# The third slot's rows turned one product group earlier, in a fused attention and routed-expert kernel

## The chip, the cores and the metric

The kernel runs on one core of one Trainium2 chip. The metric is the device time of one execution in microseconds (us); less is better. The kernel before takes 415.35 us, the median of three runs (415.18 to 416.78).

## What is computed

Attention comes first: 4 batches, 8 heads, 768 positions of 64 elements, where a position sees the first 8 positions and the last 96, with a bias that falls with the distance. Its output, 3072 rows of 512, goes into a layer of 8 experts. Each row goes to the one expert with the largest logit:

```python
logits = x @ w_gate + modality_bias[modality_id]
e_idx = np.argmax(logits, axis=1)
...
for e in range(E):
    mask = e_idx == e
    h = np.maximum(x[mask] @ w1[e], 0.0)
    out[mask] = gate_w[mask, None] * (h @ w2[e])
```

w1 of an expert is 512 x 1024, w2 is 1024 x 512, all in float32.

## The kernel before

**Slots.** After attention the rows are worked on in eight slots, one after the other (`for u in range(nslot)`, line 1733). A slot is a set of rows that share an expert: `e0` and `e1` have 4 blocks of 128 rows, then come `p0` (4 blocks, the third slot, u = 2), `g0` (1), `p1` (4), `g1` (1), `p2` (4) and `u0` (2). Since float32 products are made of three products of rounded numbers, every operand is held as a high half and a low half (`xh`, `xl` for the rows, `ah`, `al` for w1, `bh`, `bl` for w2, `hh`, `hl` for the hidden layer).

**Groups.** A slot of four blocks has eight product groups, g = 0 to 7. In `l1` (line 799) a group makes 128 of the 1024 hidden columns for all 512 rows: 12 matmuls of 128x512 into one bank `ph` (lines 826 to 828), then ScalarE makes `hh` of it (line 829) and VectorE `hl` (line 830). In `l2` (line 841) the same hidden columns are multiplied by w2: 12 matmuls into four banks `po` (lines 854 to 856). The loop puts `l2` of a group behind `l1` of the next one, so TensorE does `l1(g)`, `l2(g-1)`, `l1(g+1)`, `l2(g)`, and so on. Banks for `ph` alternate between two (`p_x`, line 84).

**Rows for the next slot.** The rows come from HBM by indirect transfers that GpSimd issues (`gather_q`, line 700, issued at line 716): 128 rows x 128 columns each, four for a block, 16 for a slot. Two are issued at each `move()`. A block, once there, goes through two steps. `turn` (line 763) is one VectorE transpose of 32x32 squares, from `xg` to `xf`. `halves_of` (line 769) is one ScalarE rounding to `xh` (line 774) and one VectorE subtraction to `xl` (line 775). All four blocks of `xh` and `xl` must be there before the first group of the slot, because each of its matmuls takes all 512 rows.

**Order.** TensorE, ScalarE and VectorE run in the order in which the program is written (`manual_schedule`, lines 1429 and 1431). In a group the loop writes, among others: `l1` with its `hh` and `hl`; two splits of weights into halves (`run(2)`, lines 751 and 757); `l2` of the group before; and at its end `fill(u, g)` (line 1662), which turns and halves the next slot's blocks. So what `fill` writes in group g stands in ScalarE's and VectorE's queues ahead of `hh`, `hl` and the splits of group g + 1. The last group of a slot has two splits of w1 for the next slot's second half (`ahp010`, `ahp011` and their low halves here).

**The few rows.** During `e1` a small product for a handful of rows of another expert runs as well: `few_t` (VectorE transpose `xTf`), `few_l1` (`phf`, 32 short matmuls in group 6, followed by `hrf` on ScalarE), `few_ht` (`htf`, two transposes on TensorE in group 7, followed by `hTf`), and `few_l2` (`pof`, in group 1 of `p0`).

Of the kernel before, what the change touches and what calls it, by code (L numbers as in the profile page):

```python
# [38 lines left out]
NE, NPS, NUS, NGR = 2, 3, 1, 2  # L39
# [30 lines left out]
def moe_attention_kernel(  # L70
# [599 lines left out]
    def ld_x(s):  # L670
        n = P * s.nt
        so = nc.sync.value_load(s.o_src, min_val=0, max_val=E * NT)
        s.ui = idp.tile([P, 4, IDW], I32, tag="ui", name=f"ui{s.name}")
        ins = nc.sync.dma_start(s.ui[:, 0 : s.nt, :], ids[ds(so, n), :].rearrange("(p t) o -> p t o", t=s.nt))
        return ins

    def ld_q(s):
        n = P * s.nt
        so = nc.sync.value_load(s.o_src, min_val=0, max_val=E * NT)
        s.uq = idq.tile([P, 4, 4, IDW], I32, tag="uq", name=f"uq{s.name}")  # L680
        src = ids[ds(so, n), :].rearrange("(g i t) o -> i g (t o)", g=4, t=s.nt)
        for b in range(4):
            nc.sync.dma_start(
                s.uq[M * b : M * b + M].rearrange("p g t o -> p g (t o)")[:, :, 0 : s.nt * IDW], src
            )
# [77 lines left out]
    def turn(s, t):  # L763


        s.xf[t] = mp.tile([P, 4, 4, M], F32, tag="xf", name=f"xf{s.name}{t}", bufs=5)
        V.transpose(s.xf[t], s.xg[:, t, :].rearrange("p (g c j) -> p c g j", g=4, c=4))

    def halves_of(s, t):
        if t == 0:  # L770
            x_hl(s)
        xf = s.xf.pop(t).rearrange("p c g i -> p c (g i)")
        sl = slice(t * P, (t + 1) * P)
        nc.scalar.copy(s.xh[:, :, sl], xf)  # L774
        V.tensor_tensor(s.xl[:, :, sl], xf, s.xh[:, :, sl].bitcast(F32), ALU.subtract)
# [84 lines left out]
    def few_in(s):  # L860
        so = nc.sync.value_load(s.o_src, min_val=0, max_val=E * NT)
        s.ui = idp.tile([P, 2], I32, tag="uif", name="uif", bufs=1)
        for g in range(4):
            nc.sync.dma_start(s.ui[M * g : M * g + M, :], ids[ds(so, M), 0:2])
# [755 lines left out]
    def load_on():  # L1620
        nonlocal nload
        while nload - nfree < NRAW and nload < 8 * len(order):
            i = nload
            with tc.issue_after(v_last[0].ins):
                ld_w(order[i // 8], "ab"[i // 2 % 2], i // 4 % 2, i % 2)
            nload += 1
# [35 lines left out]
    def fill(u, g):  # L1662

        s = order[u]
        nx = order[u + 1] if u + 1 < len(order) else None
        if u or g:
            next(bg, None)
        if len(order) == NE and len(slist) == NPS + NUS + NGR and not writes:

            order.extend(slist[j] for j in ORDER)  # L1670
            nx = order[u + 1]
        while ahead[0] < min(len(order), u + 4):
            ld_x(order[ahead[0]])
            if ahead[0] == NE:
                few_in(fs[0])
                ld_q(order[NE])
            ahead[0] += 1
        load_on()
        if ahead[1] < min(ahead[0], u + (3 if u < NE else 4)):
            s2 = order[ahead[1]]  # L1680
            if s2.rows:
                gathers.extend((gather_x, s2, t) for t in range(s2.nt))
            else:
                if ahead[1] > NE:
                    ld_q(s2)
                gathers.extend((gather_q, s2, t, g) for t in range(2 * (ahead[1] < NE), s2.nt) for g in range(4))
            if ahead[1] == NE:
                gathers.insert(len(gathers) - 8, (few_x, fs[0]))
            ahead[1] += 1
        if nx is not None and s.nt == 4:  # L1690
            first = (0, 4)[u] if u < NE else 2
            if first < g <= first + nx.nt:
                next_rows(u, (g - first - 1,), halves_of)
            if first <= g < first + nx.nt:
                next_rows(u, (g - first,), turn)
            if g + 1 == s.groups < first + nx.nt + 1:
                next_rows(u, (nx.nt - 1,), halves_of)
            if nx.nt == 1 and g > 3:
                turn(order[u + 2], g - 4)
                if g == 7:  # L1700
                    order[u + 2].mx = mx[u % 2]
                    for t in range(4):
                        halves_of(order[u + 2], t)
# [14 lines left out]
    def next_rows(u, ts, *fs_):  # L1718

        nx = order[u + 1]  # L1720
        nx.mx = mx[(u + 1) % 2]
        for f in fs_:
            for t in ts:
                assert nx.got > t
                f(nx, t)
# [7 lines left out]
    for u in range(nslot):  # L1733
        s = order[u]
        per = s.groups // 2
        for g in range(s.groups):
# [6 lines left out]
            nx = order[u + 1] if u + 1 < len(order) else None  # L1743
# [25 lines left out]
            if not u or 0 < g < 7:  # L1769
                move()  # L1770
            fill(u, g)
            if s.nt == 1 and g:
                run(2)
# [116 lines left out]
```

## Time and profile before

| what | us |
|---|---|
| median of three runs | 415.35 |
| lowest and highest run | 415.18, 416.78 |
| the profiled execution, its own time | 414.16 |
| its span, from the first to the last instruction | 412.3 |
| TensorE busy in the span | 394.3 |
| VectorE, ScalarE, GpSimd busy | 267.2, 228.7, 190.0 |

The span is 1.86 us shorter than the time of its own execution. Busy times of different engines lie beside each other, so they don't add up. Start times below count from the beginning of the span. In names, `xhp` is the tile `xh` of a `p` slot, `phe` the bank `ph` of an `e` slot, and so on; L826 is line 826. "x<-y" is what is written and what is read.

### The profile page before, as it was taken

To read this page: it belongs to the slowest core of one execution; us is meant where nothing else is said; L and a number is where in the kernel's file an instruction comes from. 1 tells how busy PE (TensorE), PEld (TensorE's weight loads), DVE (VectorE), ACT (ScalarE), POOL (GpSimd) and SP (SyncE) were. 2 spreads that over 40 slices of the span, in tenths; PEclk is the share of its full clock that TensorE was granted. 3 is DMA by queue.
4 is the path that set the end of the run, shared out by engine and by line. 5 is a ranking of instruction groups with operands and counts; after the bars stand their busy time and mean duration, and the time that the engine had idled before them with its cause. 6 is when DMAs were issued, how large, how long until landed. Compare 5 with 4: busy or idle time off the path is not lost.

```text
span 412.3 us, 10964 instructions
## 1 busy us (share of the span) xinstructions
PE 394.3 (96%) x3900; PEld 328.6 (80%) x3900; DVE 267.2 (65%) x859; ACT 228.7 (55%) x609; POOL 190.0 (46%) x334
## 2 busy tenths in 40 slices
PE   8899999999989999999997999999999999999993
PEld 6688778787877788888875888888888888888992
DVE  7899889899897598897534324488444676443220
ACT  7998889898874443263422522297232685332511
POOL 7700042276876777067770657503777340000301
PEclk9999999999999999999996999999999999999997
DMA  8999999989668762325744373449844479220201
GB/s 245 336 347 301 343 308 323 283 284 343 229 174 281 279 208 88 105 83 169 244 142 128 114 251 134 149 153 305 300 165 140 137 241 328 94 84 2 101 4 57
DMA packets 47535, 82.49 MB, mean 200 GB/s; under 512 B 11295, under 2 KB 24479, under 8 KB 47472
## 3 DMA queue, kind: packets, MB, share of 16 engines
q1 hardware_dynamic: 41296, 68.68, 51.0%
q0 software_dynamic: 5632, 12.76, 9.3%
q8 instruction: 33, 0.54, 0.5%
q10 hardware_dynamic: 544, 0.26, 0.2%
q14 instruction: 30, 0.25, 0.2%
HBM read 68.19 MB, written 13.55 MB: 198 GB/s over the span
## 4 chain that ended last, share of the span: by engine, by line
PE 80%; ACT 7%; issue 5%; DVE 4%; DMA 1%; POOL 1%; SPq 0%; POOLq 0%; DVEq 0%
ACT pr L316 6%; PE php L826 6%; PE php L827 6%; PE s L285 6%; PE php L828 5%; PE pop L855 5%; PE pop L856 5%; PE pop L854 5%; PE pt L337 5%; PE x L376 4%; PE phe L826 3%; PE poe L854 3%; PE phe L827 3%; PE poe L855 3%; PE poe L856 3%
## 5 line engine op out<-in xcount | busy, mean ns | idle before, releaser
L316 ACT ACTIVATE pr<-sc,nmx 128x168 f32<-128x168 f32 (+1 forms) x192 | 79.7, 417 | 10.1 <-DVE nmx L305 9.9
L830 DVE SCALAR_TENSOR_TENSOR hlp<-php,hhp 128x512 fp32r<-128x512 f32 x24 | 16.6, 691 | 70.1 <-ACT hhp L829 70.1
L829 ACT ACTIVATE hhp<-php 128x512 fp32r<-128x512 f32 x24 | 14.3, 598 | 80.2 <-PE php L828 80.2
L716 POOL DMA_INDIRECT xgp<-x_rows,iqp x48 | 51.4, 1071 | 15.1 <-issue 11.8
L305 DVE CUSTOM_DVE_ANT_0 sc<-s,tbl 128x168 f32<-128x168 f32 (+1 forms) x192 | 49.9, 320 | 6.7 <-PE s L285 3.9
L285 PE MATMUL s<-kb,qt 64*64 64x168 f32 (+1 forms) x768 | 40.4, 312 | 3.9 <-ACT pT L345 2.9
L954 POOL DMA_INDIRECT out<-obp,oip x12 | 14.0, 1168 | 63.9 <-ACT obp L953 61.5
L826 PE MATMUL php<-xhp,ahp 128*128 128x512 f32 x96 | 38.8, 404 | 3.0 <-ACT xhp L774 3.0
L827 PE MATMUL php<-xlp,ahp 128*128 128x512 f32 x96 | 38.5, 401 | 0.0
L828 PE MATMUL php<-xhp,alp 128*128 128x512 f32 x96 | 38.4, 400 | 0.0
L285 PEld LDWEIGHTS s<-kb,qt 64*64 64x64 f32 x768 | 28.1, 135 | 12.3 <-ACT pT L345 6.1
L855 PE MATMUL pop<-blp,hhp 128*128 128x512 f32 x96 | 37.4, 390 | 0.0
L854 PE MATMUL pop<-bhp,hhp 128*128 128x512 f32 x96 | 37.4, 390 | 0.0
L856 PE MATMUL pop<-bhp,hlp 128*128 128x512 f32 x96 | 37.4, 389 | 0.0
L316 ACT ACTIVATION_READ_ACCUMULATOR pr<-sc,nmx 128x1 f32 x192 | 36.0, 188 | 0.0
L559 POOL DMA_INDIRECT ids_sorted<-tki,pi x24 | 25.4, 1058 | 22.4 <-PE x L376 8.9
L337 PE MATMUL pt<-ident,pr 128*128 128x128 f32 x272 | 35.2, 278 | 0.0
L337 PEld LDWEIGHTS pt<-ident,pr 128*128 128x128 f32 x272 | 29.4, 141 | 3.6 <-issue 1.9
L829 ACT ACTIVATE hhe<-phe 128x512 fp32r<-128x512 f32 x16 | 9.6, 597 | 38.2 <-PE phe L828 38.2
L376 PE MATMUL x<-vx,pT 128*64 128x64 f32 x768 | 28.0, 225 | 0.8 <-ACT pT L345 0.8
L376 PEld LDWEIGHTS x<-vx,pT 128*64 128x64 f32 x768 | 24.6, 138 | 4.3 <-DMA vl<-in_v_s 1.1
L854 PE MATMUL poe<-bhe,hhe 128*128 128x512 f32 x64 | 25.3, 396 | 0.0
(392 smaller groups left out, 974.5 us busy)
## 6 DMA issues: line engine op xcount, KB each, us to landing
vx<-in_v_l SPq DMA_DIRECT2D x20, 512.0 KB
x_rows<-xr SPq DMA_DIRECT2D x48, 128.0 KB
qt<-in_q_t SPq DMA_DIRECT2D x23, 256.0 KB
kb<-in_k_t SPq DMA_DIRECT2D x6, 816.0 KB
vl<-in_v_s SPq DMA_DIRECT2D x20, 160.0 KB
rawe0a<-in_moe_w SPq DMA_DIRECT2D x4, 512.0 KB
rawe0b<-in_w SPq DMA_DIRECT2D x4, 512.0 KB
rawe1a<-in_w SPq DMA_DIRECT2D x4, 512.0 KB
```

What stands on the lines that cost most here:

```text
L285: nc.tensor.matmul(ps[h][64 * H2 : 64 * H2 + 64, s * W : s * W + w], qt[hs, hp, 64 * s : 64 * s + 64], kt[hs, hp, k0 : k0 + w], start=True ...
L305: V.tensor_tensor_reduce(out=sc, in0=pss[n, hp // 2][h][:, hp % 2 * W : hp % 2 * W + w], in1=(tbl0 if starts(n) else tbl)[:, hh, :], op0=A ...
L316: last[0] = nc.scalar.activation(pr[:, h * (PRW - W) : h * (PRW - W) + w], sc, AF.Exp, bias=nmx[:, hh : hh + 1], scale=-1.0, accum_out=sum ...
L337: pt_end[0] = nc.tensor.transpose(tp[:, i * P : (i + 1) * P], pr[:, o : o + P], ident)
L376: pv_end[0] = nc.tensor.matmul(px[h][64 * H2 : 64 * H2 + 64, o : o + D], pT[:, 64 * H2 : 64 * H2 + 64], vx[:, 0 if first else s, (2 * hp + ...
L716: ins = nc.gpsimd.indirect_dma_start(out=s.xg[:, t, g * P : (g + 1) * P], out_offset=None, in_=s.xsrc.rearrange("n (b d) -> (n b) d", b=4) ...
L826: nc.tensor.matmul(out_, hi, xh, start=(c == 0), stop=False)
L827: nc.tensor.matmul(out_, hi, xl, start=False, stop=False)
L828: pe_end[0] = nc.tensor.matmul(out_, lo, xh, start=False, stop=(c == 3))
L854: nc.tensor.matmul(s.po[t], hh[:, tt], hi, start=(fc == 0), stop=False)
L855: nc.tensor.matmul(s.po[t], hh[:, tt], lo, start=False, stop=False)
L856: pe_end[0] = nc.tensor.matmul(s.po[t], hl[:, tt], hi, start=False, stop=(fc == 7))
```

## The change

While `e1` runs (u = 1), `fill` now starts to turn the blocks of `p0` in group 3, not 4, and ends in group 6, not 7. Halves still follow their turn one group later for blocks 0 to 2 (groups 4, 5 and 6). The halves of block 3 are written right behind its turn, in group 6. No instruction is added or removed. For u = 0 and u = 2 and above the rules give the same groups as before.

```diff
         if nx is not None and s.nt == 4:
-            first = (0, 4)[u] if u < NE else 2
-            if first < g <= first + nx.nt:
+            first = (0, 3)[u] if u < NE else 2
+            at_once = u + 1 == NE
+            if first < g <= first + nx.nt - at_once:
                 next_rows(u, (g - first - 1,), halves_of)
             if first <= g < first + nx.nt:
                 next_rows(u, (g - first,), turn)
-            if g + 1 == s.groups < first + nx.nt + 1:
+            if at_once and g == first + nx.nt - 1:
                 next_rows(u, (nx.nt - 1,), halves_of)
```

ScalarE around the end of `e1`, before. In the names the digits behind `hhe1`, `xfp0` and so on are the group or the block, then a tile number; `xhp0` and `xlp0` are those of slot `p0`, `ahp010` a high half of w1.

```order
L829 ACTIVATE hhe16_4270<-phe16_4269 128x512
L896 ACTIVATE hrf_4320<-phf_4303 128x256
L774 CAST xhp0_4263<-xfp01_4267 128x4x128
L829 ACTIVATE hhe17_4333<-phe17_4332 128x512
L751 CAST ahp010_4349<-rawp0a10_4074 128x1024
L751 CAST ahp011_4353<-rawp0a11_4097 128x1024
L903 COPY hTf_4373<-htf_4370 128x256
L774 CAST xhp0_4263<-xfp02_4330 128x4x128
L774 CAST xhp0_4263<-xfp03_4377 128x4x128
L829 ACTIVATE hhp00_4382<-php00_4381 128x512
```

The same place of ScalarE's queue after the change.

```order
L829 ACTIVATE hhe16_4274<-phe16_4273 128x512
L896 ACTIVATE hrf_4324<-phf_4307 128x256
L774 CAST xhp0_4220<-xfp02_4271 128x4x128
L774 CAST xhp0_4220<-xfp03_4334 128x4x128
L829 ACTIVATE hhe17_4339<-phe17_4338 128x512
L751 CAST ahp010_4355<-rawp0a10_4074 128x1024
L751 CAST ahp011_4359<-rawp0a11_4097 128x1024
L903 COPY hTf_4379<-htf_4376 128x256
L829 ACTIVATE hhp00_4382<-php00_4381 128x512
```

The roundings of blocks 2 and 3 moved from behind `hTf` to ahead of `hhe17`. VectorE, from group 5 of `e1` on, before:

```order
L880 STREAM_TRANSPOSE xTf_4259<-xgf_4199 128x128
L775 TENSOR_TENSOR xlp0_4264<-xfp00_4218,xhp0_4263 128x4x128
L767 STREAM_TRANSPOSE xfp01_4267<-xgp0_4099 128x512
L830 SCALAR_TENSOR_TENSOR hle16_4271<-phe16_4269,hhe16_4270 128x512
L775 TENSOR_TENSOR xlp0_4264<-xfp01_4267,xhp0_4263 128x4x128
L767 STREAM_TRANSPOSE xfp02_4330<-xgp0_4099 128x512
L830 SCALAR_TENSOR_TENSOR hle17_4334<-phe17_4332,hhe17_4333 128x512
L757 TENSOR_TENSOR alp010_4350<-rawp0a10_4074,ahp010_4349 128x1024
L757 TENSOR_TENSOR alp011_4354<-rawp0a11_4097,ahp011_4353 128x1024
L775 TENSOR_TENSOR xlp0_4264<-xfp02_4330,xhp0_4263 128x4x128
L767 STREAM_TRANSPOSE xfp03_4377<-xgp0_4099 128x512
L775 TENSOR_TENSOR xlp0_4264<-xfp03_4377,xhp0_4263 128x4x128
```

And VectorE after the change, from the same point:

```order
L880 STREAM_TRANSPOSE xTf_4265<-xgf_4201 128x128
L775 TENSOR_TENSOR xlp0_4221<-xfp01_4224,xhp0_4220 128x4x128
L767 STREAM_TRANSPOSE xfp02_4271<-xgp0_4099 128x512
L830 SCALAR_TENSOR_TENSOR hle16_4275<-phe16_4273,hhe16_4274 128x512
L775 TENSOR_TENSOR xlp0_4221<-xfp02_4271,xhp0_4220 128x4x128
L767 STREAM_TRANSPOSE xfp03_4334<-xgp0_4099 128x512
L775 TENSOR_TENSOR xlp0_4221<-xfp03_4334,xhp0_4220 128x4x128
L830 SCALAR_TENSOR_TENSOR hle17_4340<-phe17_4338,hhe17_4339 128x512
L757 TENSOR_TENSOR alp010_4356<-rawp0a10_4074,ahp010_4355 128x1024
L757 TENSOR_TENSOR alp011_4360<-rawp0a11_4097,ahp011_4359 128x1024
```

Each turn moved up by one group, and the last turn and subtraction moved from behind `alp011` to ahead of `hle17`. On TensorE, GpSimd and SyncE the order of the work is the same as before.

## Rows read from the trace of the kernel before

**Rows 1.** The page: busy time per engine, and the granted clock in 40 slices.

```profile
PE 394.3 (96%) x3900; PEld 328.6 (80%) x3900; DVE 267.2 (65%) x859; ACT 228.7 (55%) x609; POOL 190.0 (46%) x334
...
PEclk9999999999999999999996999999999999999997
```

**Rows 2.** Waits of TensorE from 130 us to the end: total us, times, longest.

```profile
PE php L826 <- ACT xhp L774: 3.0, 1, 3.0
```

**Rows 3.** Stretches: us; busy PE, PEld, DVE, ACT, POOL (x count); PEclk, DMA share, GB/s.

```profile
212.00:217.90 5.90, 5.90 (x28) 4.65 (x26) 3.29 (x5) 3.38 (x5) 3.08 (x4) 1.00 0.82 235
217.90:220.90 3.00, 0.00 (x0) 0.00 (x0) 2.32 (x4) 1.51 (x3) 0.61 (x1) 0.86 0.63 187
220.90:226.50 5.60, 5.59 (x13) 4.10 (x14) 0.68 (x1) 0.00 (x0) 0.00 (x0) 0.50 0.27 87
226.50:228.00 1.50, 1.50 (x7) 1.23 (x6) 0.58 (x1) 1.02 (x2) 0.00 (x0) 0.86 0.00 0
228.00:234.00 6.00, 6.00 (x29) 4.93 (x28) 0.81 (x2) 3.90 (x7) 4.23 (x5) 1.00 0.34 131
```

**Rows 4.** Timeline of TensorE, 211 to 238 us: start, duration, [idle before <- releaser].

```profile
211.94 0.50 PE L826 MATMUL phe<-xhe,ahe 128*128 128x512 f32 x1
...
217.52 0.38 PE L901 MATMUL htf<-ident,hrf 128*128 128x128 f32 x2
220.91 0.79 PE L826 MATMUL php<-xhp,ahp 128*128 128x512 f32 x1 [3.01 <-ACT xhp L774]
221.63 0.80 PE L827 MATMUL php<-xlp,ahp 128*128 128x512 f32 x1
...
227.15 0.40 PE L856 MATMUL poe<-bhe,hle 128*128 128x512 f32 x1
...
229.45 0.39 PE L826 MATMUL php<-xhp,ahp 128*128 128x512 f32 x1
...
232.17 0.39 PE L854 MATMUL pop<-bhp,hhp 128*128 128x512 f32 x1
...
234.98 1.96 PE L912 MATMUL pof<-rawp0b,hTf 128*32 128x128 f32 x64
```

**Rows 5.** Timeline of ScalarE in the last two groups of e1.

```profile
212.38 0.61 ACT L774 CAST xhp<-xfp 128x512 fp32r<-128x512 f32 x1
...
215.54 2.00 ACT L751 CAST ahp<-rawp0a 128x1024 fp32r<-128x1024 f32 x2
...
220.24 0.62 ACT L774 CAST xhp<-xfp 128x512 fp32r<-128x512 f32 x1 [1.41 <-DVE xfp L767]
```

**Rows 6.** Timeline of VectorE in the last groups of e1.

```profile
206.10 0.65 DVE L775 TENSOR_TENSOR xlp<-xfp,xhp 128x512 fp32r<-128x512 f32 x1
...
208.16 0.69 DVE L830 SCALAR_TENSOR_TENSOR hle<-phe,hhe 128x512 fp32r<-128x512 f32 x1 [0.78 <-ACT hhe L829]
213.03 0.69 DVE L775 TENSOR_TENSOR xlp<-xfp,xhp 128x512 fp32r<-128x512 f32 x1 [4.18 <-ACT xhp L774]
213.64 0.70 DVE L767 STREAM_TRANSPOSE xfp<-xgp 128x512 f32<-128x512 f32 x1
...
219.50 0.70 DVE L767 STREAM_TRANSPOSE xfp<-xgp 128x512 f32<-128x512 f32 x1
220.89 0.69 DVE L775 TENSOR_TENSOR xlp<-xfp,xhp 128x512 fp32r<-128x512 f32 x1 [0.68 <-ACT xhp L774]
```

**Rows 7.** Timeline of GpSimd: the 8th, 12th, 13th and 16th gather for p0.

```profile
197.33 1.53 POOL L716 DMA_INDIRECT xgp<-x_rows,iqp  x1 [0.30 <-issue]
...
204.19 1.46 POOL L716 DMA_INDIRECT xgp<-x_rows,iqp  x1 [0.30 <-issue]
205.94 0.94 POOL L716 DMA_INDIRECT xgp<-x_rows,iqp  x1 [0.30 <-issue]
...
210.05 0.94 POOL L716 DMA_INDIRECT xgp<-x_rows,iqp  x1 [0.30 <-issue]
```

**Rows 8.** The tile xgp from 186 to 217 us: time from issue to landing.

```profile
DMA to landing us min/median/max: 2.4/4.1/5.9
```

## The prediction

> **What bounds the kernel now.** I read the page first. TensorE is busy for 394.3 of 412.3 us, far more than any other engine, and its clock is full in every slice but two [rows 1]: one in the middle at 6 tenths, and the last one, in which the work ends. So time is to be found only where TensorE stands still or runs at the lower clock. The waits of TensorE say where the first is: from 130 us to the end, through all eight slots, there is one wait, 3.0 us, of the first matmul of `p0` for the rounding `xhp` on ScalarE [rows 2]. The stretches around it say where the second is [rows 3]: TensorE does nothing from 217.90 to 220.90, and from 220.90 to 226.50 the granted clock is 0.50, which is 1.2 of 2.4 GHz; it is 1.00 up to 217.90 and again from 228. The middle slice at 6 tenths is this one stall and what follows it.
>
> Then the timelines, to see why `xhp` is late. `htf`, the last work of `e1` before the gap, ends at 217.90 (217.52 + 0.38) [rows 4]. The last block's turn only starts at 219.50, its rounding at 220.24, its subtraction at 220.89 [rows 5, 6]. It is late because of its place in the queues: on ScalarE two splits of w1 stand ahead (215.54 to 217.54), on VectorE their low halves do. VectorE waits for nothing right before that turn, so the rows of x are there by 219.50; how much earlier, this trace does not say.
>
> **The sum.** The stall is worth two terms.
>
> 1. The idle time: 3.01 us [rows 4].
> 2. The lower clock. From the first matmul of `p0` at 220.91 to the `poe` matmul at 227.15 there are 14 starts (12 of `l1`, two of `l2`), in 6.24 us [rows 4]. At full clock 12 starts take 232.17 - 229.45 = 2.72 us, 0.227 us each [rows 4], so 14 would take 3.18. The rest, 3.06 us, goes to the clock, and a part of it to the second matmul, which waits for `xlp`; both go when the stall goes.
>
> Together 6.07 us, if the change hides all of it. Whether it does is a question of when the last `xh` and `xl` come now. I take group 6 by its new order and the old durations.
>
> - `xhp` of block 2 takes the place that block 1 had, 212.38 [rows 5], behind `hrf`; its subtraction that at 213.03, and the last turn starts where one started before, at 213.64 [rows 6].
> - From that turn to the first matmul it took 220.91 - 219.50 = 1.41 us, and to the subtraction's end 2.08 (220.89 + 0.69 - 219.50). The last `xh` is then ready at about 215.0 and the last `xl` at 215.7.
> - The first matmul needs them at 217.75 to 217.9, when `htf` has gone through. The margin is over 2 us.
>
> What the moved work pushes back: `hhe17` and `hle17` now stand behind block 3. `phe17` ends near 215, so they slip by under 1 us, and nobody needs them before `l2` of group 7, which begins 12 matmuls after the first of `p0`, past 220. In groups 3 to 5 each turn stands ahead of `hle14`, `hle15`, `hle16`, at 0.70 us a turn; each of these is read by an `l2` only after the next group's 12 matmuls and the `l2` before it. The two splits and the two low halves of w1's second half move by about 1 us and are read four groups later. I cost all of these at nothing, under the cover of one group (some 5.4 us of TensorE, twice the 2.72 us above).
>
> One thing could not be read from the old order: the turns may wait for their gathers now, since they are asked for a group earlier and the gathers are issued at the same times. Where the trace gives a landing in this stretch, it takes 2.4 to 5.9 us [rows 8]. The 16th, issued at 210.05 [rows 7], so lands between 212.45 and 215.95. At the early end it is hidden by the subtraction before it. At the late end the last turn starts at 215.95, the first matmul's `xh` is ready at 217.36 and the last `xl` at 218.03, where the second matmul wants it at about 218.0. So both ends cost nothing, the late one just so. I take the median, 4.1 us: 214.15. The same sum for blocks 1 and 2: their last gathers start at 197.33 and 204.19 [rows 7] and land by 203.2 and 210.1 at the latest, so `hle15` and `hle16` slip by 2 to 3 us at most, still inside the cover.
>
> Where does TensorE wait next? Rows 2 show no other wait from here to the end, and what follows is fed by work that follows TensorE itself (weight loads into freed buffers, gathers spaced by matmuls), so it moves forward with it. The loads that do not are done: from 226.50 to 228.00 no transfer is active at all [rows 3], and `pof`, the first reader of the new w2 buffers, at 234.98 [rows 4], would come at 228.9. So the gain goes through to the end.
>
> The profiled execution took 414.16 us, so 408.09 after. It lies 1.19 us under the median of the runs, 415.35; against that median I predict **409.3 us**, 1.5% less. A measurement of this kernel can tell about 0.5%, or 2.1 us, from no change.
>
> One rule speaks against the cheap move. GpSimd's gather issues take 0.94 us, but 1.53 and 1.46 us where VectorE's wide subtractions of 1.2 us lie beside them; beside an `xlp` subtraction (206.10) one took 0.94 [rows 6, 7]. The Trainium skill, GPSIMD Engine Reference, section Key points, says that GpSimd shares its SBUF interfaces with VectorE and that instructions with two SBUF inputs contend with it. By that rule the earlier `xlp` subtractions would lengthen gathers too; the wide ones agree with it, the 0.94 does not.
>
> **The rivals.**
>
> *Gathers slowed by VectorE.* Before, one `xlp` lay among the gathers, at 206.10; now block 0's does too, near 199.4 (behind `hle14`). If it costs what a wide subtraction does, 1.53 - 0.94 = 0.59 us, the 16th starts at 210.64, and at the longest landing it is there at 216.54. Then the last `xl` is ready at 218.62, 0.6 us late for the second matmul: 409.9. Against it: the row with 0.94. Chance 0.05.
>
> *The clock falls all the same.* Group 6 has 32 short matmuls and group 7 two transposes, and the clock could have fallen for these. Then only 3.01 us are gained: 412.3. Against it: the clock is 1.00 all through 212.00 to 217.90, behind those short matmuls, and it is below that first in the idle stretch [rows 3]. Chance 0.07.
>
> *Nothing is gained, because the gather was the cause.* If the 16th gather lands only at 219.5, the change moves the place of the wait and no more: 415.35. Between 216 and 219.5 the gain shrinks step by step. It needs a landing of 9.4 us, against 5.9 for the longest seen; for it speaks only that the DMA engines are 0.82 busy from 212 to 217.9 [rows 3], with weights. Chance 0.09.
>
> *Slower: `phe17` held by `hle16`.* VectorE's queue has `hle16` behind the turn of block 2 now. `phe17` goes into the bank of `phe16`, which `hle16` must have read. If the 12th gather (issued 204.19) lands later than about 210.5, the turn and `hle16` (0.70 + 0.69 us) end after 211.94, where `phe17` starts [rows 4], and TensorE stands still in the middle of `e1`, 1 us for 1 us; a stall as long as the old one also brings the lower clock's 3.06 us. The old stall goes in this case too, so the time is 409.3 + 3.06 + the stall: more than 417.4, so slower by 0.5%, once the stall is over 5.1 us, at a landing of 11.4 us. With 12 us it is 418.1. Chance 0.03.
>
> **How the numbers follow.** The forecast has 0.76. Faster by over 0.5% (under 413.3) are the forecast, the slowed gathers and the clock: 0.88, less 0.01 for a clock case in which the stall goes only in part: 0.87. Within 0.5%: 0.09 + 0.01 = 0.10. Slower: 0.03. The range goes from 408.2 to 412.4. The upper end takes in the clock's rival at 412.3 and the landings between the forecast and there; the lower end lies 1.1 us under the forecast, about the distance of the profiled execution from the median, for what one execution can't show. Some 0.13 lie outside.
>
> **What would show it.** Right: no wait of `php` for `xhp`, its first matmul near 217.8, granted clock 1.00 from 212 to 234, the last turn starting between 213.6 and 216, and a span near 406.2. The time would be wrong by the rivals: a DMA wait ahead of the last turn (gathers), a clock of 0.50 with no idle time ahead of it, or a wait of `phe` for `hle` near 212. If `php` starts early and TensorE then waits elsewhere, at `pof` for w2 or at `pop` for its bank, the gain was given back later and the term that claims it goes through was wrong.

## The result, and the profile after

The changed kernel took 409.75 us, the median of four runs (408.98 to 412.01). Beside it the kernel before took 415.18, 415.35 and 416.78 us; a fourth run of it, at 2165 us, was disturbed and is left out. The ratio is 0.989, with a 95% interval from 0.9847 to 0.9933: faster by about 1%, at least 0.7%. Ratios here are those on record for the fast runs, which need not equal the ratio of the medians given beside them (0.987 here). The forecast was 409.3.

TensorE's busy time and the clock that it was granted, from the page of the changed kernel:

```profile
PE 391.6 (96%) x3900; PEld 326.9 (80%) x3900; DVE 267.5 (66%) x859; ACT 228.9 (56%) x609; POOL 190.7 (47%) x334
...
PEclk9999999999999999999999999999999999999999
```

TensorE is busy for 2.7 us less than before [rows 1], since the matmuls of the slow stretch are short again, and the middle slice at 6 tenths is gone. Asked for TensorE's waits from 130 us to the end, the trace lists none where it had one of 3.0 us [rows 2]. The same place by stretches (columns as in rows 3):

```profile
212.00:217.90 5.90, 5.90 (x42) 4.47 (x35) 1.40 (x2) 1.35 (x3) 4.68 (x5) 1.00 0.79 248
217.90:220.90 3.00, 3.00 (x16) 2.37 (x15) 2.67 (x4) 2.82 (x5) 1.24 (x2) 1.00 0.09 25
220.90:226.50 5.60, 5.60 (x27) 4.62 (x26) 1.68 (x2) 3.33 (x5) 3.60 (x4) 1.00 0.69 240
```

TensorE is busy through all of them, at 2.4 GHz. Its timeline:

```profile
211.01 1.93 PE L887 MATMUL phf<-rawp0a,xTf 128*32 128x256 f32 x32
...
218.45 0.38 PE L901 MATMUL htf<-ident,hrf 128*128 128x128 f32 x2
218.58 0.48 PE L826 MATMUL php<-xhp,ahp 128*128 128x512 f32 x1
218.90 0.44 PE L827 MATMUL php<-xlp,ahp 128*128 128x512 f32 x1
...
221.96 0.39 PE L856 MATMUL poe<-bhe,hle 128*128 128x512 f32 x1
...
229.76 1.95 PE L912 MATMUL pof<-rawp0b,hTf 128*32 128x128 f32 x64
```

Against rows 4: from `htf` to the first `php` it was 3.39 us and is 0.13; from there to the third `poe` it was 6.24 and is 3.38. That is 3.26 + 2.86 = 6.12 us. From `phf` to `pof`, which takes in both, it was 24.90 us (210.08 to 234.98) and is 18.75: 6.15 gained. The span fell by 5.1 only (412.3 to 407.2), because this execution was 0.9 us late before the change begins to act: its first matmul of the experts started at 129.3 us, that of before at 128.4. From there to the last start of L854 in slot `u0` (bank `pou`) it was 276.6 us and is 270.4, 6.2 less, so nothing was given back behind the place up to there; the tail behind it took 0.2 us more. These two distances, **the local one** (`phf` to `pof`) and **the expert part** (first `phe` to last `pou`), are what the experiments are read by, since the time ahead of them varies from execution to execution (129.3 against 128.4 us here).

### The profile page after: what moved, and what is told of

It is laid out like the page before. It is cut to its first block, busy times and chain, and to the rows that moved or that the text cites. A ratio compares the mean times of both kernels' runs of the same rounds, so it can differ in the third digit from the quotient of the medians.

```text
span 407.2 us, 10964 instructions
## 1 busy us (share of the span) xinstructions
PE 391.6 (96%) x3900; PEld 326.9 (80%) x3900; DVE 267.5 (66%) x859; ACT 228.9 (56%) x609; POOL 190.7 (47%) x334
## 4 chain that ended last, share of the span: by engine, by line
PE 83%; ACT 7%; issue 5%; DVE 2%; POOL 1%; POOLq 0%; DVEq 0%
ACT pr L316 6%; PE s L285 6%; PE pt L337 5%; PE php L826 5%; PE php L827 5%; PE php L828 5%; PE pop L856 5%; PE pop L854 5%; PE pop L855 5%; PE x L376 5%; PE phe L826 4%; PE poe L854 4%; PE phe L828 4%; PE phe L827 4%; PE poe L856 4%
## 5 line engine op out<-in xcount | busy, mean ns | idle before, releaser
L826 PE MATMUL php<-xhp,ahp 128*128 128x512 f32 x96 | 37.8, 393 | 0.0
L827 PE MATMUL php<-xlp,ahp 128*128 128x512 f32 x96 | 37.4, 390 | 0.0
L828 PE MATMUL php<-xhp,alp 128*128 128x512 f32 x96 | 37.4, 390 | 0.0
L854 PE MATMUL pop<-bhp,hhp 128*128 128x512 f32 x96 | 37.4, 389 | 0.0
L559 POOL DMA_INDIRECT ids_sorted<-tki,pi x24 | 24.3, 1012 | 21.9 <-PE x L376 8.9
L826 PE MATMUL phe<-xhe,ahe 128*128 128x512 f32 x64 | 25.3, 395 | 0.0
```

The lines of the kernel that those rows point to most:

```text
L826: nc.tensor.matmul(out_, hi, xh, start=(c == 0), stop=False)
L827: nc.tensor.matmul(out_, hi, xl, start=False, stop=False)
L828: pe_end[0] = nc.tensor.matmul(out_, lo, xh, start=False, stop=(c == 3))
L854: nc.tensor.matmul(s.po[t], hh[:, tt], hi, start=(fc == 0), stop=False)
```

## The experiments

Two theories. **Queue:** the last block's turn and halves came late because of where they stood in the order, and any order that puts them early enough gains the same. **Gather:** the rows decide, and the change gains because, or as long as, the last gather lands in time. Inside the queue theory it was open which work ahead of block 3 held it up.

The runs are in three sets, each on one chip with the kernel before beside it. On two of the chips the kernel before took 451 us instead of 415 (engines there stand still at many places for which the profile shows no releaser), so a time is compared only inside its set. The first set (before: 451.02) is the first four below.

**The change again**, six runs.

> The changed kernel once more, with more runs beside the kernel before. Theory (stall of 3.01 us and the lower clock behind it, 3.06 us, both gone): 6.1 us less, ratio 0.985, with the first matmul of p0 right behind the two transposes htf. Rival (a part of the gain is given back in some runs because the last gather lands late): ratio near 0.990, runs spread over 3 us, and a lower mean clock in the longer ones.

Measured: 444.91, ratio 0.9888 [0.9831, 0.9944], local distance 18.66. The first `php` starts at 239.71, right behind `htf` at 239.57. The gain is there on a chip on which the kernel takes 9% longer. The times alone could not tell the two expectations apart: the ratio lies near that of the rival, the runs spread over 13 us with a lower clock in the longer ones, but the kernel before spread over 12 us there as well. It is the trace, of the shortest of the six, that shows nothing given back at this place.

**Block 3's halves in their own group**, the turns early as in the change.

```diff
-            at_once = u + 1 == NE
+            at_once = False
```

> Turns one group earlier as in the change, but the halves of block 3 stay in the next group (group 7), behind hTf on ScalarE and behind the two low halves of w1 on VectorE. Theory (what counts is where the last halves stand in those two queues): the last rounding ends near 218.9 and the last subtraction near 219.6 on the clock of the kernel before, against 217.75 and 218.0 when TensorE wants them, so a stall of 1.2 us and one of 0.7 us, too short for the clock to fall: 4.2 us less than before, ratio 0.990. Rival (earlier turns are enough): 6.1 us less. Second rival (any stall there brings the clock down): 1.1 us less.

**Only the splits moved**: the kernel before, with the two splits of group 7 behind `fill`.

```diff
-                run((2 if u else 1) if s.nt > 1 else 2 * (1 - g))
+                if (u, g) != (NE - 1, 7):
+                    run((2 if u else 1) if s.nt > 1 else 2 * (1 - g))
...
+            if (u, g) == (NE - 1, 7):
+                run(2)
```

> The kernel before, with its old turns, but in group 7 of e1 the two splits of w1 (ahp010, ahp011 and their low halves) are written behind the last turn and halves. Rival, as the prediction told it (the splits ahead of the rounding are the cause): the last rounding moves up to about 218, and 5 us are gained. Theory now: on ScalarE the rounding of block 2 stands behind hTf as well, and hTf waits for htf on TensorE until 217.9, so the chain from there (rounding, subtraction, turn, rounding) starts no earlier than before: no gain, within 0.5 us of before.

**Splits and `hTf` moved**: the same, with `few_ht` too behind `fill`, ahead of the splits.

> As the run with the splits behind the last halves, but few_ht (htf and hTf) is written behind them too, so that the roundings of group 7 wait for neither. Theory: rounding of block 2 at 215.6, last turn at 216.9, last rounding done at 218.3, last subtraction at 219.0; the first two matmuls of p0 are late by some 0.6 and 1.0 us, the clock stays up: 5 us less than before, ratio 0.988, although every turn is in its old group. Rival (the earlier turns themselves bring the gain): no gain.

Measured: the halves in their own group 0.9927 [0.9889, 0.9966]; the splits alone 0.9986 [0.9945, 1.0026]; splits and `hTf` 0.9932 [0.9895, 0.9969]. The splits alone gain nothing that could be told (at most 0.55% by the interval). ScalarE of that run shows why:

```profile
239.62 0.60 ACT L829 ACTIVATE hhe<-phe 128x512 fp32r<-128x512 f32 x1 [0.38 <-PE phe L828]
242.51 0.37 ACT L903 COPY hTf<-htf 128x256 f32<-128x256 f32 x1 [2.28 <-PE htf L901]
242.78 0.62 ACT L774 CAST xhp<-xfp 128x512 fp32r<-128x512 f32 x1
244.78 0.62 ACT L774 CAST xhp<-xfp 128x512 fp32r<-128x512 f32 x1 [1.38 <-DVE xfp L767]
```

and TensorE, behind `htf` at 242.09:

```profile
245.45 0.50 PE L826 MATMUL php<-xhp,ahp 128*128 128x512 f32 x1 [2.98 <-ACT xhp L774]
```

With the splits gone ScalarE is free at 240.2 and then stands 2.28 us at `hTf`, which waits for `htf`, the last thing that TensorE does before the gap. Block 2's rounding stands behind it, then block 2's subtraction, block 3's turn and its rounding. From `hTf` to the first `php` that chain is 2.94 us. The trace of before has the same chain, at the end of ScalarE's queue:

```profile
217.93 0.37 ACT L903 COPY hTf<-htf 128x256 f32<-128x256 f32 x1 [0.39 <-PE htf L901]
218.20 0.62 ACT L774 CAST xhp<-xfp 128x512 fp32r<-128x512 f32 x1
```

There too `hTf` waited for `htf`, and from it to `php` it is 2.98 us [rows 4]. ScalarE had come to the end of the splits 0.39 us before it could go on. So on ScalarE the stall is the length of a chain that begins with TensorE's own last work; a shorter queue ahead of `hTf` can't shorten it.

VectorE had a hold of its own that ended at the same moment. In the trace of before:

```profile
216.62 2.36 DVE L757 TENSOR_TENSOR alp<-rawp0a,ahp 128x1024 fp32r<-128x1024 f32 x2 [0.25 <-ACT ahp L751]
218.90 0.69 DVE L775 TENSOR_TENSOR xlp<-xfp,xhp 128x512 fp32r<-128x512 f32 x1
```

The low halves of the splits end at 218.98, and block 2's subtraction starts right with their end, while its rounding was done at 218.82. So moving `hTf` alone would have gained next to nothing too: the rounding could have begun at 217.54, behind the splits, but the subtraction not before 218.90. That is an estimate from these rows; no run moved `hTf` alone.

In the other two of this set the chip's own gaps hid what was asked. ScalarE of the run with the halves in their own group, for instance:

```profile
241.41 0.60 ACT L829 ACTIVATE hhe<-phe 128x512 fp32r<-128x512 f32 x1 [3.58 <-PE htf L901]
```

By the order this waits for `phe17` alone, which ended near 238; it came over 3 us later, and the same happened in the run with splits and `hTf` moved (241.08). Both then stalled for over 3 us. So both were run again, in the second set, on a chip where the kernel before took 414.84.

**The halves in their own group, again.**

> The kernel with early turns and block 3's halves in group 7, once more, since ScalarE's instructions of that group came late in its first trace (hhe17 started 3 us behind its matmuls). Theory, on a trace without such gaps: last rounding done at about 218.9 on the clock of the kernel before, last subtraction at 219.6, stalls of 1.2 and 0.7 us ahead of the first two matmuls of p0, clock full behind them: 4.2 us less than before, ratio 0.990. Rival (earlier turns are enough): ratio 0.985. Second rival (the short stall brings the clock down too): ratio 0.997.

Measured: 411.68, ratio 0.9912 [0.9878, 0.9947], local distance 20.44, so 4.46 gained of 6.15. TensorE:

```profile
221.68 0.50 PE L826 MATMUL php<-xhp,ahp 128*128 128x512 f32 x1 [0.98 <-ACT xhp L774]
222.44 0.50 PE L827 MATMUL php<-xlp,ahp 128*128 128x512 f32 x1 [0.26 <-DVE xlp L775]
```

Block 2 is past `hTf` here. Block 3's rounding is still behind it (220.74), and its subtraction, at 221.71, right behind the low halves: 0.94 us from `hTf` to the first `php`, 0.98 us of wait. The granted clock is 1.00 in every stretch from 212 to 232.

**Splits and `hTf` moved, again.** No turn is earlier than before in this one.

> The kernel with old turns, and the two splits and few_ht written behind the last halves, once more for the same reason (hhe17 3.2 us late in the first trace). Theory: the first two matmuls of p0 are late by some 0.6 and 1.0 us, the clock stays up: 5 us less than before, ratio 0.988. Rival (the earlier turns themselves bring the gain): ratio 1.000.

Measured: 411.63, ratio 0.9919 [0.9895, 0.9942], local distance 19.83, 5.07 gained.

```profile
222.85 0.50 PE L826 MATMUL php<-xhp,ahp 128*128 128x512 f32 x1 [0.40 <-ACT xhp L774]
223.58 0.50 PE L827 MATMUL php<-xlp,ahp 128*128 128x512 f32 x1 [0.23 <-DVE xlp L775]
```

Its last turn, on VectorE, waits for no transfer:

```profile
221.45 0.70 DVE L767 STREAM_TRANSPOSE xfp<-xgp 128x512 f32<-128x512 f32 x1
```

Most of the gain comes without asking for the rows one group sooner, by place in the queues alone; so the last gather was not what bounded the kernel before. By whole times this set gained less than by the local distance: 3.2 us of 4.46 in the run above, 3.2 of 5.07 in this one, 5.35 of 6.24 in the next. The kernel before was not traced on this chip, and where the rest went is not shown.

**Only blocks 2 and 3 in group 6**: the first turn in group 4 as before, and the last two blocks turned and halved in group 6. Against the change:

```diff
-            first = (0, 3)[u] if u < NE else 2
+            first = (0, 4)[u] if u < NE else 2
...
-            if at_once and g == first + nx.nt - 1:
-                next_rows(u, (nx.nt - 1,), halves_of)
+            if at_once and g == 6:
+                next_rows(u, (2,), halves_of)
+                next_rows(u, (3,), turn)
+                next_rows(u, (3,), halves_of)
```

(With the bounds of the two conditions between made to fit.)

> Turns and halves of blocks 0 and 1 in their old groups, blocks 2 and 3 turned and halved in group 6, so only what stood in group 7 is moved. Theory (only what stood behind hTf and the low halves matters): the chain of group 6 is hrf, rounding of block 1 at 213.3 on the clock of the changed kernel, turn of block 2 at 214.6, last turn at 216.7 (when the last gather lands), last subtraction done at 218.8: as good as the change, ratio 0.985 to 0.989. Rival (all four blocks must move for the gain): ratio over 0.995.

Measured: 409.49, ratio 0.9865 [0.9833, 0.9898], no wait of `php`, local distance 18.66, 6.24 gained. As good as the change, without touching groups 3 to 5: what counts is that the last two blocks stand ahead of group 7's splits and of `hTf`. This run passes both at once, so it does not tell one from the other. VectorE there:

```profile
217.28 0.71 DVE L767 STREAM_TRANSPOSE xfp<-xgp 128x512 f32<-128x512 f32 x1
218.67 0.69 DVE L775 TENSOR_TENSOR xlp<-xfp,xhp 128x512 fp32r<-128x512 f32 x1 [0.69 <-ACT xhp L774]
```

The last turn starts 5.56 us behind `phf` (5.68 in the change) and waits for no transfer, and the subtraction ends at 219.36, before the matmul that reads it (219.61).

**The last gathers held up.** The change, with two clearings of an unused 128x2048 tile on GpSimd ahead of block 3's gathers.

```diff
+        if (s.name, t, g) == ("p0", 3, 0):
+            held = mp.tile([P, 2048], F32, name="held")
...
+            for _ in range(2):
...
+                    hold = nc.gpsimd.memset(held, 0.0)
```

In the trace one clearing runs ahead of the four gathers and the other between the second and the third.

> The change, with two memsets of 128x2048 on GpSimd's queue ahead of the last gathers of p0 (a memset of 128x256 took 0.32 us, so some 2.3 us each, an estimate by length): nothing is left out. In the changed kernel's trace the last subtraction ended 0.1 us ahead of the matmul that reads it. Theory (no margin is left, the last gather's landing now sets the start of p0): a stall of some 4 us ahead of p0, behind it a granted clock of 0.50, so the whole gain is lost: ratio 0.998 to 1.005. Rival (over 2 us of margin, as the prediction had it): a stall of under 2.5 us, ratio near 0.992.

Measured: 413.92, ratio 0.996 [0.992, 1.0001]; local distance 22.87 (4.12 of 6.15 lost), expert part 274.5 against 270.4 (4.1 lost). The clearings took 1.83 and 1.82 us, less than I had put them at, so the 16th gather started at 215.38, 3.93 us behind `phf` against 0.66 in the change, and the stall was about half of that expected. VectorE and TensorE (line numbers are 18 higher in this kernel):

```profile
219.71 0.71 DVE L785 STREAM_TRANSPOSE xfp<-xgp 128x512 f32<-128x512 f32 x1 [4.62 <-DMA xgp<-x_rows,iqp]
...
221.10 0.69 DVE L793 TENSOR_TENSOR xlp<-xfp,xhp 128x512 fp32r<-128x512 f32 x1 [0.68 <-ACT xhp L792]
```

```profile
221.12 0.49 PE L844 MATMUL php<-xhp,ahp 128*128 128x512 f32 x1 [1.86 <-ACT xhp L792]
221.85 0.51 PE L845 MATMUL php<-xlp,ahp 128*128 128x512 f32 x1 [0.23 <-DVE xlp L793]
```

The stretches behind the stall in this run:

```profile
221.00:224.00 3.00, 2.64 (x7) 1.91 (x8) 2.75 (x4) 2.73 (x5) 0.88 (x2) 0.70 0.09 27
224.00:227.00 3.00, 3.00 (x12) 2.37 (x11) 0.94 (x2) 0.65 (x2) 0.00 (x0) 0.73 0.65 217
227.00:230.00 3.00, 3.00 (x15) 2.49 (x14) 0.65 (x1) 2.68 (x4) 1.78 (x2) 1.00 0.53 195
```

Now the gather does bind, and a wait of 1.86 + 0.23 us brings the granted clock down, to a mean of 0.70 and 0.73 over six microseconds. Of the 4.12 us lost 2.09 are waits; the rest, 2.0 us, goes to the clock for the most part (in the second run with the halves in their own group, at full clock, 1.24 us of waits cost 1.7). The gather theory is right about the changed kernel once its last gather is some 3 us late.

The third set (before: 450.56) asked how much late is too late.

**The change once more**, six runs, for the others to be compared with.

> The changed kernel once more. From the first matmul of e0 to the last start in pou it took 270.4 us, the kernel before 276.6. Theory: again 270.4, since the whole gain lies in that part, and a ratio of 0.985 to 0.989; what differs between runs lies ahead of it, in attention. Rival (part of the gain is given back in some runs by late gathers): over 271.5 in that part.

Measured: 443.13, ratio 0.9754 [0.9668, 0.9839], local distance 18.63. The expert part is 284.0 us there, with that chip's gaps in it, so the number that I had expected for it could not come. The ratio is better than the 0.985 to 0.989 that I expected; the local distance is that of the first set within 0.03 us, so the excess lies elsewhere and is not explained.

**One clearing instead of two**, one run.

> The change, with one memset of 128x2048 on GpSimd's queue ahead of the last four gathers of p0 (such a memset took 1.83 us); nothing is left out. Theory (the landing of the last gather sets the start of p0, with 0.1 us to spare in the changed kernel): the last turn starts some 1.8 us later, the first two matmuls of p0 wait some 1.3 and 0.4 us, the clock stays up as it did behind a wait of 0.98 us: 272.1 us from the first matmul of e0 to the last start in pou. Rival (margin of 2 us): 270.4. Second rival (the clock falls for this wait too): 273.5 or more.

Measured: 440.15, local distance 19.21 against 18.63, and a wait of only 0.23 us before the second matmul. The loss that I expected did not come, but this says little: the last turn (236.87) did not wait for its gather, because `hrf` ahead of the chain came late by one of the chip's gaps. Inconclusive.

**Two clearings ahead of block 2's gathers**, one run: the slower rival, `phe17` held by `hle16` behind block 2's turn.

> The change, with two such memsets ahead of the gathers of block 2 (3.7 us), so that blocks 2 and 3 land late; nothing is left out. This makes the slower rival's case: the turn of block 2 waits, hle16 stands behind it on VectorE, and phe17 needs the bank that hle16 reads. Theory: block 2 lands near 212, hle16 ends near 213.5 on the changed kernel's clock, and phe17 waits under 1.5 us for it; then the last block is late as well: 274 to 276 us from the first matmul of e0 to the last start in pou. Rival (hle16's cover of a group holds): no wait of phe, 274.5 as with both memsets ahead of block 3.

Measured: 446.52, local distance 20.91, 2.3 more than the change. VectorE, and TensorE's `phe17`:

```profile
233.99 0.71 DVE L785 STREAM_TRANSPOSE xfp<-xgp 128x512 f32<-128x512 f32 x1 [2.98 <-DMA xgp<-x_rows,iqp]
234.62 0.65 DVE L848 SCALAR_TENSOR_TENSOR hle<-phe,hhe 128x512 fp32r<-128x512 f32 x1
...
241.14 0.71 DVE L785 STREAM_TRANSPOSE xfp<-xgp 128x512 f32<-128x512 f32 x1 [2.46 <-DMA xgp<-x_rows,iqp]
```

```profile
235.33 0.50 PE L844 MATMUL phe<-xhe,ahe 128*128 128x512 f32 x1
...
242.56 0.49 PE L844 MATMUL php<-xhp,ahp 128*128 128x512 f32 x1 [1.27 <-issue]
```

Block 2's turn came 0.74 us after `phf` started, where in the change it is 1.84 ahead of it; `hle16` ended at 235.27 and `phe17` began right then, 2.08 us behind `phf`, where it is 1.86 or 1.87 in the change and in the other three traces of this set. The profile lists no wait for it, but the times fit the mechanism, and 2.6 us of lateness brought it 0.2 us. Most of the rest of the loss is the old stall in small, from the last block (1.27 + 0.23 us of wait). With 2.3 us lost of about 6 gained, it is still no loss against the kernel before.

**The index of the next slot moved** behind the last gather of `p0`: the changed kernel, where `iqg`, a small GpSimd product, stands ahead of block 3's last three gathers.

> The change, with the index arithmetic of g0 on GpSimd (iqg, line 708, which lay between two gathers of block 3 and took 1.43 us in the changed kernel) behind the last gather of p0. Theory: the last gather is issued and lands some 1.2 us earlier, which only adds margin: 270.4 us in the part from e0 to pou, no wait of p0, ratio 0.985 to 0.989. Rival (late landings cost the changed kernel part of its gain): shorter than the changed kernel by 0.5 us or more.

Measured: 440.25, ratio 0.9802 [0.973, 0.9874], against 0.9754 [0.9668, 0.9839] for the change; local distance 18.66 against 18.63. The last turn still waited 0.55 us for its gather, TensorE for nothing. No difference that could be told; `iqg` had taken only 0.37 us in the change of this set, so there was little to gain by moving it.

## Why the prediction was right, and where not

**The two terms.** Right, and each nearly in size: 3.01 of idle time became 3.26 by starts (from `htf` to `php`), 3.06 of lower clock became 2.86; in sum 6.07 forecast, 6.12 measured, 6.15 over the local distance. The change hides all of it.

**The gain goes through to the end.** Right: 6.15 us at the place, 6.2 over the expert part, and no wait of TensorE behind it.

**The cause.** Half right. The place in the queues was the cause, as the runs show in which the last blocks pass the splits and `hTf`, or these two are moved; but the prediction named only the two splits of w1 that "stand ahead" on ScalarE, and their low halves on VectorE. The run that moved just these gained nothing. What held block 2's rounding was `hTf`, and so TensorE itself; row 217.93, with its wait for `htf`, stood in the trace of before and I left it out [rows 5]. The low halves were a hold as well, on the subtraction, and ended within 0.2 us of the other; by these rows either one alone was enough for the stall. The forecast came out all the same, because its sum places both blocks by the new order, in group 6, where they are past the splits, the low halves and `hTf` alike; for the sum it did not matter which of them had held them.

**The margin.** The step that failed: "The margin is over 2 us", and with it the median landing. VectorE of the changed kernel:

```profile
209.17 0.70 DVE L767 STREAM_TRANSPOSE xfp<-xgp 128x512 f32<-128x512 f32 x1
209.79 0.65 DVE L830 SCALAR_TENSOR_TENSOR hle<-phe,hhe 128x512 fp32r<-128x512 f32 x1
213.96 0.69 DVE L775 TENSOR_TENSOR xlp<-xfp,xhp 128x512 fp32r<-128x512 f32 x1 [3.52 <-ACT xhp L774]
216.69 0.71 DVE L767 STREAM_TRANSPOSE xfp<-xgp 128x512 f32<-128x512 f32 x1 [2.04 <-DMA xgp<-x_rows,iqp]
218.09 0.69 DVE L775 TENSOR_TENSOR xlp<-xfp,xhp 128x512 fp32r<-128x512 f32 x1 [0.69 <-ACT xhp L774]
```

The last turn waited 2.04 us for its gather. The last subtraction ended at 218.78, and the matmul that reads it started at 218.90: 0.1 us. Moved back by this execution's 0.93 us the turn is at 215.76, where the landing's late end had been put at 215.95; "the late one just so" was the case that came, and my choice of the median was too good by 1.6 us. That the whole stall went with 0.1 us to spare was luck in part. GpSimd, and the tile's landings from 186 to 217 us, tell of what:

```profile
206.05 0.94 POOL L716 DMA_INDIRECT xgp<-x_rows,iqp  x1 [0.30 <-issue]
207.07 1.43 POOL L708 TENSOR_SCALAR iqg<-uqg,pdiv 128x4 int32<-128x4 int32 x1
208.78 1.34 POOL L716 DMA_INDIRECT xgp<-x_rows,iqp  x1 [0.27 <-issue]
210.42 0.94 POOL L716 DMA_INDIRECT xgp<-x_rows,iqp  x1 [0.30 <-issue]
211.67 0.94 POOL L716 DMA_INDIRECT xgp<-x_rows,iqp  x1 [0.30 <-issue]
...
214.16 1.30 POOL L716 DMA_INDIRECT xgg<-x_rows,iqg  x1 [0.30 <-issue]
```

```profile
DMA to landing us min/median/max: 2.6/4.7/7.2
```

The 16th gather starts 0.66 us after `phf`, where it started 0.03 ahead of it: 0.69 later [rows 7]. Its rows are there 5.0 us after that, inside the range forecast, though the longest of the stretch is now 7.2 where it was 5.9 [rows 8].

The larger part of the 1.6 us is the landing, and the trace of before could have told it. Rows 8 has only two landings in it, of the gathers issued at 194.25 and at 205.94, so its median is no more than their mean:

```profile
DMA to landing us min/median/max: 5.9/5.9/5.9
DMA to landing us min/median/max: 2.4/2.4/2.4
```

They flew under different loads (columns as in rows 3):

```profile
192.00:198.00 6.00, 6.00 (x29) 4.95 (x28) 2.87 (x4) 2.60 (x3) 4.78 (x5) 1.00 0.95 343
204.00:209.90 5.90, 5.90 (x28) 4.75 (x26) 4.07 (x6) 1.64 (x3) 4.61 (x5) 1.00 0.17 44
```

The 16th gather flies where the DMA share is 0.82 before and 0.79 after, so the long landing was the one to expect. In the traces of before, after and the second set every landing that is listed of `p0`'s gathers bears this out: 5.9 to 7.4 us where the DMA share was 0.75 or more while it was under way, 2.4 to 3.6 us where it was 0.54 or less.

**The rivals.** *Gathers slowed by VectorE* is half true: the two gathers that start inside an `xlp` subtraction (208.59 to 209.24, and 213.96 to 214.65) take 1.34 and 1.30 us instead of 0.94. The Trainium skill's rule on shared SBUF interfaces (GPSIMD Engine Reference, Key points) so holds for `xlp` too; the 0.94 that I set against it was of a gather that had started 0.16 us before its subtraction. The rival's price, 0.59 us on the 16th, was close to the 0.69 measured, but by luck. The 0.69 is made up mainly of `iqg`, 1.16 us longer, and the 14th gather, 0.35 longer, less 0.34 and 0.52 for the 8th and the 12th, which had lain beside wide subtractions before; block 0's `xlp`, at 200.33, lengthened none. It cost nothing, because the landing was 5.0 us and not the 5.9 that the rival reckoned with. *The clock falls all the same* did not happen: 1.00 through all stretches. *The gather was the cause* is refuted by the run without earlier turns, whose last turn waited for no transfer and which gained 5.07 us. *Slower* was far off: `hle16` ended at 210.44, 2.4 us before `phe17` started, and holding block 2 up by 2.6 us cost 0.2. (Its sum for a landing of 12 us gives 418.0, not 418.1, which changes nothing.)

## What to carry to other kernels

When an engine stands still for a chain of work on other engines, follow the chain back through each queue that it passes, and note when each hold there ends. Here two holds ended together: on ScalarE an instruction that waited for the stalled engine's own last work, on VectorE two wide subtractions. Taking away the one that was easy to see gained nothing; the blocks had to get past both. For that it was enough to move two blocks, not a whole schedule. When work is moved ahead of a transfer that it used to follow, size the landing by transfers that flew under the same DMA load, since the transfer's cover is what the move uses up.

## What I had not expected of the hardware

The clock came down behind waits of TensorE of 3.01 us (kernel before), 2.98 + 0.22 us (only the splits moved: means of 0.78 and 0.65 over the next 6 us) and 1.86 + 0.23 us (last gathers held up), and stayed at 1.00 behind 1.27 + 0.23, 0.98 + 0.26 and 0.40 + 0.23 us. So the price of lateness is far from even: 2.09 us of waits cost 4.12, and 1.24 us cost 1.7 (20.44 against 18.75).

An indirect gather of 128 rows took 2.4 to 3.6 us to land while the DMA engines were little busy and 5.9 to 7.4 us while they were loaded, as told above.

The small product `iqg` on GpSimd took 1.43 us beside VectorE's wide subtractions, and 0.27 in the trace of before, where it started at 206.97, beside a turn. And the same kernel took 415 us on one chip and 451 on others, with gaps whose cause the profile does not show; the change's gain held wherever it was measured (ratios 0.9888, 0.9754 and 0.989), but of the traces from the slower chips only some could be read.
